# Four dense blocks in plain float32, merged complex products and moved reloads in a gated mix of an S4 convolution and a dense layer

## The chip, the core and the metric

The kernel runs on one core of a Trainium2 chip. Its engines are TensorE (PE), VectorE (DVE), ScalarE (ACT), GpSimd (POOL) and SyncE (SP); each runs its own instructions in order, and they wait for each other by semaphores. SP, ACT and POOL also issue transfers, which 16 DMA engines carry out. The metric is the device time of one execution in microseconds (us), the median of several.

## The reference

Two branches work on inputs of 2048 rows by 512 channels and are mixed by a gate for each row. Branch a is an S4 convolution: per channel a kernel K of 2048 taps is made from 128 complex modes and convolved with the input. Branch b is a dense layer of 512 to 1792 to 512 with a tanh gelu.

```python
dt = jnp.exp(log_dt)[:, None]
P = jnp.exp((dt * (A_re + 1j * A_im))[:, :, None] * l)       # 512 x 128 x 2048
K = jnp.einsum("dn,dnl,dn->dl", Cc, P, dt * Bc).real
a = causal_convolution(K, u) + u * Dskip                     # by rfft/irfft of length 4096
h = gelu(x @ w1 + b1)                                        # 2048 x 1792
b = h @ w2 + b2
g = sigmoid((u * gate_w).sum(-1, keepdims=True))
return g * a + (1 - g) * b
```

All is float32.

## The kernel before

The program has two parts. **The front** holds three streams. *Dense* (`hidden`, `output`): the 2048 rows are 8 tiles of 256 rows (`SB`), the 1792 hidden columns are 14 blocks of 128 in two halves of 7, and each tile is passed twice, once for each half; 64 steps in all. A matmul operand in float32 is split into a high half in float32r (`xh`, `wh`, `hh`: a cast by ACT or DVE) and a low half (`xlo`, `wl`, `hl`: a subtraction by DVE), and three products stand for one: high by high, low by high, high by low. The first weights wait in `sk` and `y`, buffers which the taps need later. `wh0`/`wl0` number k are the halves of the first layer's block k, `wh1`/`wl1` those of the second layer's. *Taps* (`prepare`, `coefficients`, `powers`, `magnitudes`, `rotate`, `contract`): powers of the modes are built by doubling in groups of 32 channels, 4 units of 4 groups, mostly on DVE, and contracted on PE; a first stage of the transform follows and the results go to DRAM (`tk_d`). *Signal*: the same first stage for the input, in 8 steps, to `tu_d`.

The order of the front is made by a small planner: each stream adds tasks with an engine, a length and what they read and write; a due number for each task decides which of the ready ones an engine takes next. The table `DUE` holds these numbers, the constants ahead of it shape the due times of the streams, and the planner's result is the order in which each engine's instructions stand in the program. `late` collects output products that are left for the second part.

**The convolution** (`conv`) comes after the front, in code order: 16 steps of `taps`, `signal`, `product`, `inverse`, `turn`. ACT copies the result of a step to `sa`, SP stores it to DRAM (`t4_d`), and after each 8 of the 32 slabs (a group) they are read back transposed into `den` and `t3`. Some of these reloads are held back in the list `held` and issued in a later step. `dense(k, queue)` reads a pair of tiles of the dense result back from DRAM, at the steps in `TIMES`, and `gated` multiplies it by its gate. At the end `rest` makes the leftover output products, and for each of eight tile pairs in `ORDER` the last matmuls (`pb`) are made from `den` or `t3`, added to the dense result and stored. PE reads tile pairs 0 and 1 from `den`, the others from `t3`; pairs 6 and 7 need the columns 16 to 24 of `t3`, pairs 4 and 5 the columns 8 to 16.

```python
if h == 24 and g < 2:
    held.append((t3[g:P:4, 16:24], rows[:, 24:32]))
    continue
if h > 8 and g == 2:
    held.append((t3[g:P:4, h - 8 : h], rows[:, h : h + 8]))
```

Of the kernel before, what the change touches and what calls it, by code (L numbers as in the profile page):

```python
# [33 lines left out]
T_0 = 30.908  # L34
T_MLP = 394.521
K_0 = 37.384
T_KG = 348.964
U_0 = 18.366
U_GAP = 16.805
LAG = 11.668  # L40
TABLE = 22.276
D_KA = -39.446
D_KP = 49.119
D_S1 = -141.104
D_EV = -12.266
D_H = -43.84
D_LO = -40.918
# [9 lines left out]
T_EARLY, T_LOFT, T_DEN = 111.918, -38.088, 66.187
Y_K, Y_U = 38.596, 37.383
W_MLP = (-0.038, -0.0445, 0.0156)
W_KG = (-0.0539, -0.0324, -0.0092)  # L60
W_U = (-0.0055, -0.1406, -0.0062)
D_MAG = -1.67
D_ROT = 0.254
D_CON = -215.721
D_PHA = 0.435
D_PRE = 0.748
D_XL = -38.576
D_COE = -209.658
D_OUT = -128.426
D_DTB = -9888.799  # L70
D_D0A = -91.29
D_LAST = -87.539
# [1 line left out]
D_KA0 = 171.664
D_DT = 8.244
D_PRM = -152.302
D_D0 = 46.196
D_WAVE0 = -326.561
D_COE0 = -59.569
D_SP1 = -888.307  # L80
D_G0 = 111.914
D_GW = 1362.531
D_XS0 = 96.565
T_PRE = 284.272
W_CAST = (0, 0, 0, 1, 1, 0, 1, 0, 0, 1, 0, 1, 0, 0)
# [1447 lines left out]
```

## Time and profile before

| | before |
|---|---|
| median of 3 runs | 504.18 us (502.92 to 505.89) |
| profiled execution, its own time | 504.54 us |
| its span | 502.8 us |
| busy: PE, DVE, ACT, POOL | 485.5, 426.9, 356.5, 71.4 us |
| DMA | 116.58 MB, mean 232 GB/s |
| granted TensorE clock, mean | 0.984 |

The span runs from the first instruction to the last; the profiled execution took 1.7 us more than it. A row of a timeline is start, length, engine, line of the program, operation, output and inputs, and in brackets the idle time before it and what ended that. SPq, ACTq are the sequencers of these engines, which issue transfers. A matmul's length is longer than the distance to the next one's start, since matmuls are pipelined. A plain float32 matmul shows as two rows. A row of a group has the number of instructions, the time they cover and the mean of one in ns.

### The profile page before, as it was taken

The numbers are of one execution on the slowest core, as the hardware profiler recorded it, in microseconds if no ns is written. First come the engines' busy times: TensorE is split into PE (matmuls) and PEld (weight loads), VectorE is DVE, ScalarE is ACT, GpSimd is POOL, SyncE is SP. The second block draws the span as 40 slices with busy tenths as digits, with TensorE's granted clock in tenths as the row PEclk, the third lists the DMA queues.
The fourth block names the chain that finished last, engine by engine and source line by source line (L and its number), as shares of the span: only waits on it lengthen the run. The fifth ranks groups of instructions, "written<-read, shape, count | busy, mean of one in ns | idle before, by whom it ended". The sixth has DMA issues, their size and how long they took to land.

```text
span 502.8 us, 12225 instructions
## 1 busy us (share of the span) xinstructions
PE 485.5 (97%) x4798; PEld 377.9 (75%) x4798; DVE 426.9 (85%) x793; ACT 356.5 (71%) x647; POOL 71.4 (14%) x115
## 2 busy tenths in 40 slices
PE   6999999999999999999999999999999989999976
PEld 5998898898898888989879888988988822223622
DVE  6999999999999999998999999999820269999234
ACT  4999768799884969977587996576533657889113
POOL 1012022101020101201221110011020040121003
PEclk8899999999999999999999999999999999999978
DMA  8977999955789625988973558795557999999867
GB/s 288 389 196 184 300 251 245 304 156 147 162 260 225 170 85 109 273 214 207 261 188 44 189 87 190 181 312 158 181 186 169 258 346 393 354 412 367 332 236 265
DMA packets 85001, 116.58 MB, mean 232 GB/s; under 512 B 39900, under 2 KB 41456, under 8 KB 84400
## 3 DMA queue, kind: packets, MB, share of 16 engines
q1 hardware_dynamic: 74880, 86.54, 53.5%
q0 software_dynamic: 9680, 27.04, 24.3%
q10 hardware_dynamic: 384, 2.23, 1.3%
q8 instruction: 37, 0.61, 0.5%
q14 instruction: 20, 0.16, 0.1%
HBM read 65.97 MB, written 49.81 MB: 230 GB/s over the span
## 4 chain that ended last, share of the span: by engine, by line
PE 60%; DVE 15%; DMA 9%; ACT 8%; issue 4%; SPq 3%; POOL 1%; DVEq 0%; ACTq 0%
PE pk L831 7%; PE ph L1023 7%; PE ph L1025 7%; PE ph L1024 6%; PE acc L1068 6%; PE p2k L1268 6%; PE acc L1069 5%; PE acc L1070 5%; PE pb L1426 3%; PE pa L1307 3%; DVE y L794 3%; DVE y L806 2%; PE p2u L1268 2%; DMA t_d<-sa 2%; PE ph L537 2%
## 5 line engine op out<-in xcount | busy, mean ns | idle before, releaser
L1023 PE MATMUL ph<-xh,wh 128*128 128x256 f32 x448 | 129.0, 288 | 3.1 <-ACT wh L932 3.0
L1025 PE MATMUL ph<-xh,wl 128*128 128x256 f32 x448 | 127.9, 286 | 0.9 <-DVE wl L934 0.9
L1024 PE MATMUL ph<-xlo,wh 128*128 128x256 f32 x448 | 127.7, 285 | 0.0
L1023 PEld LDWEIGHTS ph<-xh,wh 128*128 128x128 f32 x448 | 86.2, 192 | 9.5 <-issue 3.8
L1024 PEld LDWEIGHTS ph<-xlo,wh 128*128 128x128 f32 x448 | 86.3, 193 | 2.0
L1025 PEld LDWEIGHTS ph<-xh,wl 128*128 128x128 f32 x448 | 86.2, 192 | 1.4 <-DVE wl L934 1.4
L1068 PE MATMUL acc<-wh,hh 128*128 128x512 f32 x206 | 83.0, 403 | 0.0
L1069 PE MATMUL acc<-wl,hh 128*128 128x512 f32 x206 | 81.0, 393 | 0.0
L1070 PE MATMUL acc<-wh,hl 128*128 128x512 f32 x206 | 80.5, 391 | 0.0
L1040 ACT ACTIVATE ph<-ph,b1t 128x256 f32<-128x256 f32 x112 | 50.6, 452 | 32.4 <-PE ph L1025 30.5
L831 PE MATMUL pk<-y,den 128*32 128x64 f32 x2048 | 61.6, 290 | 0.1
L831 PEld LDWEIGHTS pk<-y,den 128*32 128x32 f32 x2048 | 57.2, 136 | 3.8 <-issue 2.1
L1053 DVE TENSOR_TENSOR hl<-ph,hh 128x512 fp32r<-128x512 f32 (+1 forms) x62 | 38.5, 622 | 24.3 <-ACT hh L1043 21.4
L1068 PEld LDWEIGHTS acc<-wh,hh 128*128 128x128 f32 x206 | 38.7, 188 | 18.6 <-issue 8.8
L794 DVE TENSOR_TENSOR y<-y,ea 128x64 f32<-128x64 f32 (+4 forms) x80 | 45.6, 570 | 1.4 <-ACT y L784 1.0
L1070 PEld LDWEIGHTS acc<-wh,hl 128*128 128x128 f32 x206 | 38.7, 188 | 8.7
L1069 PEld LDWEIGHTS acc<-wl,hh 128*128 128x128 f32 x206 | 38.7, 188 | 6.0
L1043 ACT CAST hh<-ph 128x512 fp32r<-128x512 f32 (+1 forms) x62 | 33.1, 533 | 13.7 <-PE acc L1069 11.9
L637 DVE TENSOR_TENSOR loft<-den,zz 128x256 f32<-128x256 f32 (+2 forms) x48 | 37.5, 780 | 0.2
L638 DVE TENSOR_TENSOR loft<-den,zz 128x256 f32<-128x256 f32 (+2 forms) x48 | 37.4, 779 | 0.1
L806 DVE TENSOR_TENSOR y<-y,loft 128x2048 f32<-128x2048 f32 x16 | 36.7, 2292 | 0.6 <-ACT loft L755 0.5
L1098 POOL DMA_DIRECT2D out_dram<-b2b x16 | 14.3, 913 | 100.8 <-DMA out_dram<-io 99.3
(188 smaller groups left out, 889.9 us busy)
## 6 DMA issues: line engine op xcount, KB each, us to landing
tu_d<-attic SPq DMA_DIRECT2D x64, 128.0 KB, 4.8
tk_d<-sk SPq DMA_DIRECT2D x32, 256.0 KB, 5.2
t_d<-sa SPq DMA_DIRECT2D x32, 256.0 KB, 5.7
tk<-tk_d SPq DMA_DIRECT2D x24, 256.0 KB, 5.0
t<-t_d POOLq DMA_DIRECT2D x9, 512.0 KB, 7.5
attic<-in_xt_dram SPq DMA_DIRECT2D x16, 256.0 KB, 5.2
xh_d<-xh SPq DMA_DIRECT2D x8, 512.0 KB, 5.9
xl_d<-xlo SPq DMA_DIRECT2D x8, 512.0 KB, 7.1
```

The lines of the kernel that those rows point to most:

```text
L794: nc.vector.tensor_mul(both(n, 64 - 3 * n, n), both(0, 64 - n, n), an)
L806: v.tensor_mul(y[:, 0].rearrange("p (a b) c -> p a b c", a=2), e.rearrange("p (a b) c -> p a b c", a=2), cc,)
L831: nc.tensor.matmul(pks[q][32 * j : 32 * j + 32, :, gg], x[:, r, :, ch], y[:, r, :, ch], start=(r == 0), stop=(r == 1), skip_group_check=True,)
L1023: nc.tensor.matmul(p, h, xh[xk][:, d], start=(d == 0), stop=False)
L1024: nc.tensor.matmul(p, h, xlo[xk][:, d], start=False, stop=False)
L1025: nc.tensor.matmul(p, lo, xh[xk][:, d], start=False, stop=(d == 3))
L1040: nc.scalar.activation(phs[q][:, n], phs[q][:, n], AF.Gelu_apprx_tanh, bias=b1t[:, f : f + 1])
L1053: nc.vector.tensor_sub(lo, phs[q][:, 0:nf], hi.bitcast(F32))
L1068: nc.tensor.matmul(a, h, wh[1][w], start=start, stop=False)
L1069: nc.tensor.matmul(a, h, wl[1][w], start=False, stop=False)
L1070: nc.tensor.matmul(a, l, wh[1][w], start=False, stop=(j == 3))
L1268: nc.tensor.matmul(out[64 * i : 64 * i + 64], w, x, start=True, stop=True)
```

## The change

1. *Plain float32.* For the first tile and the first four hidden blocks (`N_RAW = 4`), PE multiplies the loaded x and w1 as they are: 16 matmuls of 256 columns in float32 in place of 48 in float32r. The splits of these weights stay, since later tiles need them. The first weights of blocks 0 and 1 are loaded on ACT's queue.
2. *Merged products.* A complex product was four DVE operations (two products, a difference, a sum). `turned` makes it two, a product of twice the size and a sum of twice the size; for that `zz` is kept in four versions, two of which ACT copies (once as it is, once negated). `zz` moves to `shed`.
3. *Magnitudes from four powers.* ACT makes ten powers in `ea` where there were six, and copies seven columns to `y` where it was one; two of five doublings on DVE go.
4. *New front order.* New constants and a new `DUE`, now a plain sequence of ranks.
5. *Two reload pairs behind the loop.* The two held reloads of group 2, which POOL issued in steps 13 and 14, and the dense reads of the last two pairs (`THERE`), which SP issued in steps 13 and 14, go behind the loop, one pair on SP and one on ACT; the other dense reads come one or two steps earlier.

```diff
-TIMES = (5, 6, 7, 8, 10, 12, 13, 14)
+TIMES = (4, 5, 6, 7, 8, 10)
...
-    -100494, -3354, -2435, -1656, -1201, -1858, 2786, 719, 214, 1100, 242, -2033, -2824, 689, -3674, -3295, -2780,
+    1, 14, 16, 18, 20, 22, 24, 26, 30, 33, 41, 44, 47, 43, 79, 81, 93, 94, 99, 110, 119, 124, 128, 131, 136, 133, 4,
...
+        def turned(due, dst, a, b, n, t, ka, kd, kt):
+
+            w = a.shape[-1]
+            m = n * w
+            z = bass.AP(a.tensor, a.offset, [a.ap[0], [0, 2], *a.ap[1:]])
+            b = b.rearrange("p (b c) w -> p b c w", b=2).unsqueeze(3).to_broadcast([P, 2, 2, n, w])
+            t = t[:, : 4 * m].rearrange("p (b c n w) -> p b c n w", b=2, c=2, w=w)
+            v = t[:, 1, 1].copy()
+            v = bass.AP(v.tensor, v.offset, [v.ap[0], [-m, 2], *v.ap[1:]])
+            vec(4 * m, lambda: nc.vector.tensor_mul(t, z, b), due, [ka, "zz"], kt)
+            vec(2 * m, lambda: nc.vector.tensor_add(dst, t[:, 0], v), due, kt, [kd])
...
-                for k in range(11):
-                    e = ea[u % 2][:, k] if k < 6 else eb[:, k - 6]
-                    nc.scalar.activation(e, sc[:, 0], AF.Exp, scale=float(2**k))
+                for k, m in enumerate((32, 33, 34, 35, 3, 2, 1, 4, 8, 16, 64, 128, 256, 512, 1024)):
+                    e = ea[u % 2][:, k] if k < 10 else eb[:, k - 10]
+                    nc.scalar.activation(e, sc[:, 0], AF.Exp, scale=float(m))
...
+            def again():
+                nc.scalar.copy(zz[:, 1], zz[:, 0])
+                nc.scalar.mul(zz[:, 3], zz[:, 2], -1.0)
...
-                cmul(
-                    t, x[:, :, n : 2 * n], x[:, :, 0:n], zz[:, 0, i, cs], zz[:, 1, i, cs], n,
-                    xt_[:, :, 0:n], xv_[:, :, 0:n], ("xc", k), ["zz"], ("xc", k), "xt", "xv",
+                turned(
+                    t, x[:, :, n : 2 * n], x[:, :, 0:n], zz[:, :, i, cs], n,
+                    loft, ("xc", k), ("xc", k), ["xt", "xv"],
                 )
...
+            def copies():
+                nc.scalar.copy(e[:, 0:4], ea[u % 2][:, 0:4, cs])
+                nc.scalar.copy(e[:, 60:63], ea[u % 2][:, 4:7, cs])
...
-            for k in range(5):
+            for k in range(2, 5):
                 vec(2 * CW << k, lambda k=k: double(k), t, [("ea", u % 2)], ["y1"])
...
+            def plain(n, f):
+                for d in range(4):
+                    x, w = plainx[d // 2][0], rooms0[f][:, 0, d * P : (d + 1) * P]
+                    x = x[:, d % 2 * SB : d % 2 * SB + SB]
+                    nc.tensor.matmul(phs[q][:, n], w, x, start=(d == 0), stop=(d == 3))
...
+                if b == 0 and f < N_RAW:
+                    t_ = mm(
+                        1.74, lambda n=n, f=f: plain(n, f), t,
...
+            for f in range(2):
+                pl.add(
+                    "ACT", 0.4, lambda f=f: nc.scalar.dma_start(room[f][:, 0], w_rows(f, 0)), -3000 + f,
+                    [], [("room", f, 0)], lat=0.0, wire=(256 / 360.0, IN),
+                )
...
-            if s in (9, 10, 13, 14):
+            if s in (9, 10):
                 to, rows = held.pop(0)
                 nc.gpsimd.dma_start(to, rows)
...
             if s in TIMES:
-                dense((*HERE, *THERE)[TIMES.index(s)], nc.sync)
+                dense(HERE[TIMES.index(s)], nc.sync)
             if s > 9:
                 gated(HERE[s - 10])
+        for (to, rows), on, k in zip(held[::-1], (nc.sync, nc.scalar), THERE):
+            on.dma_start(to, rows)
+            dense(k, on)
```

How the instructions move is seen best in three places. Numbers behind a name are its buffer; `ph` holds hidden blocks before the gelu, `acc` output products, `attic` the loaded x, `sk` and `y` the loaded weights.

First, PE's row at its start, before: a warm-up, then the first hidden block in three products.

```order
L1526 UNCONDITIONAL_BRANCH
L1147 MATMUL pk0_91<-dm_147 128x128 x13
L1023 MATMUL ph0_88<-xh00_106,wh00_110 128x256
L1024 MATMUL ph0_88<-xlo00_108,wh00_110 128x256
L1025 MATMUL ph0_88<-xh00_106,wl00_124 128x256
```

The same place after:

```order
L1157 MATMUL pk0_91<-dm_146 128x128 x13
L1020 MATMUL ph0_88<-attic_76,sk_94 128x256 x8
L1020 MATMUL ph1_89<-attic_76,sk_94 128x256 x8
L1071 MATMUL acc1_87<-wh10_116,hh0_137 128x512
L1072 MATMUL acc1_87<-wl10_130,hh0_137 128x512
L1073 MATMUL acc1_87<-wh10_116,hl0_140 128x512
```

The four plain blocks stand first, and output products come directly behind them; before, five hidden blocks in three products stood ahead of the first output product.

Second, DVE's row at its start, before, behind the split of x:

```order
L934 TENSOR_TENSOR wl10_131<-sk_94,wh10_117 128x512
L612 TENSOR_TENSOR pr_101<-loft_77 128x128
L668 TENSOR_TENSOR pr_101<-pr_101 128x512
L934 TENSOR_TENSOR wl00_124<-sk_94,wh00_110 128x512
L673 TENSOR_SCALAR pr_101<-pr_101 128x128
L934 TENSOR_TENSOR wl01_125<-sk_94,wh01_111 128x512
L930 CAST wh11_118<-sk_94 128x512
L934 TENSOR_TENSOR wl11_132<-sk_94,wh11_118 128x512
```

After, from the end of the split of x on:

```order
L923 TENSOR_TENSOR xlo00_107<-attic_76,xh00_105 128x512
L923 TENSOR_TENSOR wl13_133<-sk_94,wh13_119 128x512
L586 CAST loft_77<-loft_77 128x128
L923 TENSOR_TENSOR wl11_131<-sk_94,wh11_117 128x512
L587 TENSOR_TENSOR pr_100<-loft_77 128x128
L919 CAST wh02_111<-sk_94 128x512
L655 TENSOR_TENSOR pr_100<-pr_100 128x512
L923 TENSOR_TENSOR wl02_125<-sk_94,wh02_111 128x512
L660 TENSOR_SCALAR pr_100<-pr_100 128x128
L1056 TENSOR_TENSOR hl0_140<-ph0_88,hh0_137 128x512
L919 CAST wh03_112<-sk_94 128x512
L923 TENSOR_TENSOR wl10_130<-sk_94,wh10_116 128x512
```

The splits of the first-layer weights 0 and 1 (wl00, wl01) now stand ahead of that of x, and wl10, which the second output product reads, is the last of these rows.

Third, SP's row at the end of the convolution, before:

```order
L1343 DMA loft_77<-out_0_dram 128x2x512
L1315 DMA t4_d_61<-sa4_4827 64x2x512
L1315 DMA t4_d_61<-sa5_4828 64x2x512
L1343 DMA loft_77<-out_0_dram 128x2x512
L1315 DMA t4_d_61<-sa0_4823 64x2x512
L1315 DMA t4_d_61<-sa1_4824 64x2x512
L1446 DMA out_0_dram<-attic_76 128x2x512 x3
```

After:

```order
L1325 DMA t4_d_61<-sa4_4690 64x2x512
L1325 DMA t4_d_61<-sa5_4691 64x2x512
L1325 DMA t4_d_61<-sa0_4686 64x2x512
L1325 DMA t4_d_61<-sa1_4687 64x2x512
L1419 DMA t3_4662<-t4_d_61 32x4096
L1353 DMA loft_77<-out_0_dram 128x2x512
L1459 DMA out_0_dram<-attic_76 128x2x512 x3
```

The last four stores have no dense read between them any more; a reload of group 2 and a dense read follow them.

ACT's row at the same place, before, with the reloads of the last group:

```order
L1313 COPY sa0_4823<-pa150_5416 128x512
L1313 COPY sa1_4824<-pa151_5419 128x512
L1330 DMA den_78<-t4_d_61 32x2048 x2
L1330 DMA t3_4799<-t4_d_61 32x4096 x3
L1349 ACTIVATE loft_77<-loft_77,gate_69 128x512 x2
```

After:

```order
L1323 COPY sa0_4686<-pa150_5275 128x512
L1323 COPY sa1_4687<-pa151_5278 128x512
L1340 DMA den_78<-t4_d_61 32x2048 x2
L1340 DMA t3_4662<-t4_d_61 32x4096 x3
L1359 ACTIVATE loft_77<-loft_77,gate_69 128x512 x2
L1419 DMA t3_4662<-t4_d_61 32x4096
L1353 DMA loft_77<-out_0_dram 128x2x512
```

The other held reload and the last dense read stand behind the five reloads of the last group.

More of the change, by code (lines that the diff above doesn't have):

```diff
@@ L33 @@
 NB = 2 * NSB
[L34 to L47, printed above, removed]
+T_0 = 33.369
+T_MLP = 397.0
+K_0 = 47.904
+T_KG = 342.331
+U_0 = 5.566
+U_GAP = 16.682
+LAG = 13.265
+TABLE = 0.0
+D_KA = -86.428
+D_KP = 95.084
+D_S1 = 29.729
+D_EV = -42.828
+D_H = -112.395
+D_LO = -48.166
 PS = (2, 3, 1, 2)
 N_ACC, N_H, N_PK, N_PU = PS
-D_SP = 5.602
-D_UL, D_UN, D_UA = -95.479, -24.453, -6.871
+D_SP = 21.319
+D_UL, D_UN, D_UA = -61.72, -46.925, -171.918
 MEM = (6, 2, 3)
 N_LD, N_HL, N_ST = MEM
-D_XS = 12.979
+D_XS = 21.116
 D_G = 2.936
 N_WARM = 13
[L57 to L72, printed above, removed]
-N_REST = 3
[L74 to L85, printed above, removed]
+T_EARLY, T_LOFT, T_DEN = 178.612, -1083.199, 54.393
+Y_K, Y_U = 27.579, 43.389
+W_MLP = (-0.0414, -0.046, 0.0184)
+W_KG = (-0.0406, -0.0643, 0.0065)
+W_U = (0.026, -0.1004, 0.0029)
+D_MAG = -21.881
+D_ROT = -73.254
+D_CON = -826.122
+D_PHA = -0.328
+D_PRE = 56.826
+D_XL = -13.443
+D_COE = -18.746
+D_OUT = -86.704
+D_DTB = -3780.088
+D_D0A = 19.191
+D_LAST = -7.801
+N_REST = 3
+D_KA0 = 22.676
+D_DT = 17.298
+D_PRM = -1055.059
+D_D0 = -39.205
+D_WAVE0 = -217.107
+D_COE0 = -75.159
+D_SP1 = -335.755
+D_G0 = 63.045
+D_GW = 739.44
+D_XS0 = 137.591
+T_PRE = 38.862
+W_CAST = (1, 0, 0, 0, 1, 1, 1, 0, 1, 0, 0, 0, 1, 1)
 X_CAST = (1, 1, 1, 1)
-D_X0, D_B2, D_B2A, D_DM = -2266.733, -4.442, -32.871, 35.72
+D_X0, D_B2, D_B2A, D_DM = -122.333, -53.659, 114.804, 136.838
 N_G = 9
+N_RAW = 4
 N_ATTIC, N_LOFT, N_TK = 11, 8, 10
@@ L297 @@
 TURN_PE = 0.095
-SLOW = 1.18
+SLOW = 1.0
 class Clock:
@@ L390, in run @@
                 took, (before, behind) = t.wire
-                wire = max(wire, at + before) + took * (SLOW if at > 22.0 else 1.6 if 3.2 < at < 4.2 else 1.15)
+                wire = max(wire, at + before) + took * (SLOW if at > 2.7 else 1.3)
                 end = wire + behind
@@ L457, in vec @@
         def vec(n, fn, due, reads=(), writes=(), fast=1):
-            return pl.add("DVE", 0.071 + n / 941.0 / fast, fn, due, reads, writes)
+            return pl.add("DVE", 0.064 + n / 952.0 / fast, fn, due, reads, writes)
         def act(n, fn, due, reads=(), writes=(), table=None, ops=1):
@@ L486, in front @@
         ph = pool.tile([P, 33, CW], I32, name="phase")
-        zz = pool.tile([P, 2, 5, UW], F32, name="zz")
+        zz = shed.rearrange("p k d -> p (k d)").rearrange("p (q k w) -> p q k w", q=4, w=UW)
         x4 = pool.tile([P, 2, 4, UW], F32, name="x4")
-        ea = tiles(2, [P, 6, UW], "ea")
+        ea = tiles(2, [P, 10, UW], "ea")
         pr = pool.tile([P, 7, UW], F32, name="pr")
@@ L583, in early @@
                 else:
-                    due, key = T_LOFT + m, ["xt", "xv"] if m < N_ATTIC + 4 else ["tt"] if m < N_ROOM else []
+                    due, key = T_LOFT + m, ["xt", "xv"] if m < N_ATTIC + 4 else ["tt"] if m < N_ROOM else ["zz"]
                 move(
@@ L712, in coefficients @@
             vec(5 * UW, lambda: v.tensor_mul(zz[:, 0], rr[:, 2:7], eb[:, 0:5]), t, ["xv", kx], ["zz"])
-            vec(5 * UW, lambda: v.tensor_mul(zz[:, 1], fr[:, 2:7], eb[:, 0:5]), t, ["xt", kx], ["zz"])
+            vec(5 * UW, lambda: v.tensor_mul(zz[:, 2], fr[:, 2:7], eb[:, 0:5]), t, ["xt", kx], ["zz"])
+            def again():
+                nc.scalar.copy(zz[:, 1], zz[:, 0])
+                nc.scalar.mul(zz[:, 3], zz[:, 2], -1.0)
+            act(10 * UW, again, t + D_KA, [], ["zz"], ops=2)
             t1, v1, wc = (eb[:, 2 * i : 2 * i + 2].unsqueeze(2) for i in range(3))
@@ L716, in coefficients @@
             cmul(t, x4[:, :, 0:1], wc, rr[:, 1], fr[:, 1], 1, t1, v1, kx, ["xt", "xv"], "x4", kx, kx)
-            cmul(
-                t, x4[:, :, 1:2], x4[:, :, 0:1], zz[:, 0, 0], zz[:, 1, 0], 1, t1, v1,
-                "x4", ["zz"], "x4", kx, kx,
-            )
-            t2, v2 = (
-                z.rearrange("p a b c -> p (a b c)")[:, : 4 * UW].rearrange(
-                    "p (a b c) -> p a b c", a=2, b=2
-                )
-                for z in (xt_, xv_)
-            )
-            cmul(
-                t, x4[:, :, 2:4], x4[:, :, 0:2], zz[:, 0, 1], zz[:, 1, 1], 2, t2, v2,
-                "x4", ["zz"], "x4", "xt", "xv",
-            )
+            turned(
+                t, x4[:, :, 1:2], x4[:, :, 0:1], zz[:, :, 0], 1,
+                eb.rearrange("p a w -> p (a w)"), "x4", "x4", [kx],
+            )
+            turned(t, x4[:, :, 2:4], x4[:, :, 0:2], zz[:, :, 1], 2, loft, "x4", "x4", ["xt", "xv"])
         def phases(c, t):
@@ L771, in powers @@
                 n = 1 << i
-                cmul(
-                    t, x[:, :, n : 2 * n], x[:, :, 0:n], zz[:, 0, i, cs], zz[:, 1, i, cs], n,
-                    xt_[:, :, 0:n], xv_[:, :, 0:n], ("xc", k), ["zz"], ("xc", k), "xt", "xv",
+                turned(
+                    t, x[:, :, n : 2 * n], x[:, :, 0:n], zz[:, :, i, cs], n,
+                    loft, ("xc", k), ("xc", k), ["xt", "xv"],
                 )
@@ L783, in magnitudes @@
             pl.add("GP", 0.13, lambda: nc.gpsimd.memset(e[:, 63], 1.0), t + D_KA, [], ["y1"])
-            act(CW, lambda: nc.scalar.copy(e[:, 0], ea[u % 2][:, 5, cs]), t + D_KA, [("ea", u % 2)], ["y1"])
+            def copies():
+                nc.scalar.copy(e[:, 0:4], ea[u % 2][:, 0:4, cs])
+                nc.scalar.copy(e[:, 60:63], ea[u % 2][:, 4:7, cs])
+            act(7 * CW, copies, t + D_KA, [("ea", u % 2)], ["y1"], ops=2)
             def both(lo, step, n):
@@ L1025, in products @@
                     nc.tensor.matmul(p, lo, xh[xk][:, d], start=False, stop=(d == 3))
+            def plain(n, f):
[3 more added lines that the diff above has]
+                    nc.tensor.matmul(phs[q][:, n], w, x, start=(d == 0), stop=(d == 3))
             for n, f in enumerate(fs):
                 w = f % FH
+                if b == 0 and f < N_RAW:
+                    t_ = mm(
+                        1.74, lambda n=n, f=f: plain(n, f), t,
+                        [("room", f, 0), *(key for _, key in plainx)], [("h", q)], turn="f32",
+                    )
+                    for k in [("sk", c, j) for c in range(2) for j in range(4)] if f < 4 else ("y0", "y1"):
+                        pl.readers[k].append(t_)
+                    continue
                 mm(
@@ L1105, in output @@
                         add(n, r, t)
-        kept = []
+        kept, plainx, rooms0 = [], [], []
         def add(n, r, t):
@@ L1132, in dense @@
             room = [sks[:, f] if f < 4 else ys[:, f - 4] for f in range(FH)]
+            plainx.extend(x)
+            rooms0.extend(room)
+            for f in range(2):
+                pl.add(
+                    "ACT", 0.4, lambda f=f: nc.scalar.dma_start(room[f][:, 0], w_rows(f, 0)), -3000 + f,
+                    [], [("room", f, 0)], lat=0.0, wire=(256 / 360.0, IN),
+                )
             for f in range(FH):
-                for r in range(2):
+                for r in range(f < 2, 2):
                     move(
@@ L1211, in front @@
         for t, due in zip(pl.tasks, DUE, strict=True):
-            t.due = due / 10
+            t.due = due
         for t in pl.run():
```

4 lines of the change are left out of this document (2 added, 2 removed), and 154 rows, old and new, of the table DUE.

## The prediction

> **What bounds the kernel now.** I read the page's busy times first, then the busy time by stretch, then who waited for whom, and then the timeline of the stretches where TensorE is not full.
>
> ```profile
> span 502.8 us, 12225 instructions
> PE 485.5 (97%) x4798; PEld 377.9 (75%) x4798; DVE 426.9 (85%) x793; ACT 356.5 (71%) x647; POOL 71.4 (14%) x115
> PEclk8899999999999999999999999999999999999978
> ...
> 6.00:9.20 3.20, 0.25 (x3) 0.06 (x1) 3.05 (x10) 1.24 (x2) 0.70 (x2) 0.91 1.04 383
> 9.20:15.60 6.40, 5.67 (x25) 5.37 (x26) 6.33 (x13) 5.37 (x22) 0.00 (x0) 0.51 1.05 383
> 15.60:40.00 24.40, 24.40 (x171) 22.39 (x177) 23.86 (x58) 23.87 (x35) 1.83 (x2) 1.00 0.77 253
> 40.00:100.00 60.00, 60.00 (x650) 51.06 (x638) 59.46 (x118) 45.56 (x80) 11.86 (x16) 1.00 0.97 268
> 100.00:200.00 100.00, 99.59 (x1161) 87.04 (x1154) 96.44 (x177) 82.77 (x154) 10.97 (x18) 1.00 0.65 165
> 200.00:300.00 100.00, 99.57 (x1185) 85.36 (x1184) 95.43 (x190) 81.81 (x147) 16.56 (x26) 1.00 0.74 185
> 300.00:400.00 100.00, 100.00 (x1092) 88.94 (x1091) 69.14 (x112) 56.10 (x99) 9.81 (x16) 1.00 0.75 199
> ...
> PE pb L1426 <- DMA den<-t_d: 4.3, 1, 4.3
> ...
> PE p2k L1268 <- POOL f L1251: 1.6, 1, 1.6
> ```
>
> In a stretch's row the columns are its length, the busy time of PE, weight loads, VectorE, ScalarE and GpSimd, then granted clock, DMA share and GB/s. From 15.6 to 400 us PE lacks 0.84 us in all, at full clock: there TensorE is the bound, and a shorter VectorE instruction buys nothing. What can be won lies in three places: the first 15.6 us (PE late, then at half clock), the start of the convolution at 400 us (1.6 us), and the end (4.3 us of waiting, with a half clock behind it).
>
> **The start: four blocks in plain float32.**
>
> ```profile
> GB/s 0 0 0 83 97 197 296 242 300 398 351 262 358 361 367 410 410 397 402 401 398 393 356 348 356 401 397 393 390 366 370 385 393 401 442 406 389 377 352 258
> ...
> 1.19 5.06 PE L1147 MATMUL pk<-dm 128*128 128x128 f32 x26 [1.19 <-POOL dm L1142]
> 7.80 2.02 ACT L932 CAST wh<-sk 128x512 fp32r<-128x512 f32 x3 [3.67 <-DMA sk<-in_w_dram]
> 9.21 0.58 PE L1023 MATMUL ph<-xh,wh 128*128 128x256 f32 x1 [2.97 <-ACT wh L932]
> 10.73 0.58 PE L1025 MATMUL ph<-xh,wl 128*128 128x256 f32 x1 [0.72 <-DVE wl L934]
> 15.47 0.42 DVE L930 CAST wh<-sk 128x512 fp32r<-128x512 f32 x1
> 15.64 0.28 PE L1024 MATMUL ph<-xlo,wh 128*128 128x256 f32 x1
> 15.76 0.28 PE L1025 MATMUL ph<-xh,wl 128*128 128x256 f32 x1
> 15.81 0.69 DVE L934 TENSOR_TENSOR wl<-y,wh 128x512 fp32r<-128x512 f32 x1
> 16.41 0.69 DVE L934 TENSOR_TENSOR wl<-sk,wh 128x512 fp32r<-128x512 f32 x1
> ...
> 487.29 10.49 PE L1426 MATMUL pb<-t,g1t 128*64 128x512 f32 x52
> ```
>
> *Price on PE.* A float32r matmul of 256 columns starts every 0.12 us (15.64, 15.76), so the 48 removed ones are 5.8 us. Plain float32: the last row covers six tile pairs of the end, 12 times 512 columns by a pair of 64-wide halves that run together, 0.87 us each; 256 columns of a full-width weight are then 0.44, sixteen of them 7.0 us. The change costs PE 1.2 us here.
>
> *When it can begin.* The first row is GB/s in half microseconds; summed, 1.34 MB has moved by 6.6 us. That is the step constants, x, the parameters, c1 and the first weight of before, which ScalarE could use at 7.80: landing costs 1.2 us more. After, the two first weights go out on ScalarE's queue and x on SyncE's; both x halves and both weights are done at about 1.21 MB, 6.3 us, so usable at 7.5, against 9.21 and 10.73 for the first products of before. PE would end the four blocks at 14.5.
>
> *What then holds it.* The output products that follow need the split of the second weights. On VectorE the order now has, from the first split (possible once the first weight has landed, about 5.7, and ScalarE has cast it, 6.3) to the low half wl10 that the second output matmul reads: ten 512-wide operations of 0.60 us (15.81 to 16.41), five casts of 0.34 (15.47 to 15.81), nine 128-wide ones that I put at 0.25, an estimate: 9.9 us, and 0.3 for a weight not yet there: 16.5. PE idles 1.8 us. By the same count it waits 0.9 us for wl06 and 1.2 us for wl05. So the seven hidden blocks and 24 output matmuls of the first tile (24 at 0.23, 36 at 0.12) end at 14.5 + 1.8 + 5.5 + 4.3 + 2.1 = 28.2 us. Before, 25 matmuls (3.0 us of full-clock work) were done at 15.6, and the other 12.6 us of the same work ran unbroken: 28.0. The start is worth 0: the earlier PE runs into VectorE, which splits the same weights and has two casts more. Bounds: 4.4 us gained if VectorE kept up (all waits gone); lost 1.2 us if the half clock comes back: the warm-up ends at 6.25, and in before the gap from there to 9.21 brought 0.51 from 9.2 on. Of that gap 1.25 us would be left. As long a half clock as before's (9.2 to 15.6) would end the four blocks 3.2 us later, at 17.7, 1.2 us behind wl10. I take 0, since more than half of the gap is gone.
>
> The Trainium skill (TensorE: Matmul & The Clock Gate, Part 1: The HAM clock gate) says that the gate falls to half after an idle window of about 3.4 us, and that the window is free-running. A gap of 2.96 us was enough here, so the trace is the stricter of the two; by the rule full clock stays and the sum is the same 0, with a half clock it would be the 1.2 us more.
>
> **Merged products, four powers.**
>
> ```profile
> L637 DVE TENSOR_TENSOR loft<-den,zz 128x1024 f32<-128x1024 f32 x16 | 19.6, 1225 | 0.2
> ...
> L637 DVE TENSOR_TENSOR loft<-den,zz 128x512 f32<-128x512 f32 x16 | 11.1, 692 | 0.1
> ```
>
> Doubling 512 elements adds 533 ns, so 159 ns of an operation are fixed. Each of the 56 products goes from four operations to two with the same elements: 112 x 0.159 = 18 us at most; counted by starts (0.60 for 0.69) 7 us. Two doublings fewer in 16 magnitudes save 32 short ones, 5 to 8 us. ScalarE gets 16 exponentials, 8 long copies and 16 more copies, some 12 us, at 71% busy. All of it is off PE's path (the rows above): 0, with 1.5 us either way for the new order. The switches between the two matmul kinds are 32 in both orders.
>
> **Start of the convolution.**
>
> ```profile
> 400.84 0.18 POOL L1120 COPY look<-xh 128x1 f32<-128x1 f32 x1 [23.78 <-ACT xh L1043]
> 401.15 1.72 POOL L1112 DMA_DIRECT2D out_dram<-io  x2
> 403.01 0.88 POOL L1250 TENSOR_SCALAR f<-cc 32x256 f32<-32x256 f32 x1
> 405.77 1.08 PE L1268 MATMUL p2k<-tk,f 128*64 128x512 f32 x4 [1.63 <-POOL f L1251]
> ```
>
> PE waits for matrices that GpSimd makes after two accumulating stores, which wait for a cast. In the new order one more pair of output products stands behind that cast, so it is done some 1.4 us sooner relative to PE's last hidden block, but the stores then wait for two copies behind it: GpSimd gains 0.5 us. I take 0.5; bounds 0 and 1.6.
>
> **The end.**
>
> ```profile
> 462.81 1.05 POOL L1399 DMA_DIRECT2D t<-t_d  x2
> 467.22 1.17 SPq L1315 DMA_DIRECT2D t_d<-sa  x2
> 476.60 0.39 PE L1362 MATMUL acc<-wh,hl 128*128 128x512 f32 x1
> 478.13 1.15 ACTq L1330 DMA_DIRECT2D den<-t_d  x2
> 481.25 6.22 PE L1426 MATMUL pb<-den,g1t 128*64 128x512 f32 x16 [4.26 <-DMA den<-t_d]
> ...
> 445.00:450.00 5.00, 5.00 (x40) 1.17 (x31) 5.00 (x9) 3.53 (x8) 2.62 (x5) 1.00 1.10 422
> 465.00:470.00 5.00, 5.00 (x25) 3.31 (x24) 0.86 (x2) 1.43 (x3) 0.00 (x0) 1.00 1.02 378
> 470.00:475.00 5.00, 5.00 (x23) 4.13 (x22) 0.99 (x2) 0.00 (x0) 0.00 (x0) 1.00 0.95 362
> 481.00:485.00 4.00, 3.75 (x10) 1.38 (x12) 0.78 (x2) 1.33 (x2) 0.00 (x0) 0.50 1.00 348
> ...
> t_d<-sa SPq DMA_DIRECT2D x32, 256.0 KB, 5.7
> ```
>
> The last stores are issued at 467.2, and the reload that needs them can go only at 478.13: 11 us, against a median of 5.7, because the DMA engines are full (share about 1). The change takes two reloads (2 x 0.52 MB) and two loads of the dense result (the same) out from ahead of them: 2.1 MB at 370 GB/s (mean of 378 and 362) is 5.7 us. The stores land at 472.4, or 473.5 by the median; I take 473. The first slab came 3.1 us after its issue (478.13 to 481.25): 476.1, before PE ends its leftover products (476.99, less 0.5). So the wait of 4.26 us goes, and with it the half clock (0.50): two tile pairs took 6.04 us (481.25 to 487.29) where the next six took 1.75 each, 2.5 us more. PE: 476.5 + 8 x 1.75 = 490.5, and as before 5.0 us to the end (497.78 to 502.8): 495.5. Late next is the DMA: from 472.4 on it must move 4.2 MB of reads and 4.2 MB of results, 8.4 MB at 370, 22.7 us, to 495.1, and about 1 us to close: 496.1, which I take. ScalarE's fifth and later reloads wait for landings on shared semaphores, which at these rates are there.
>
> The Trainium skill (DMA: Bandwidth & Descriptors, Specifications) gives about 358 GB/s as HBM's limit for a core. By it the end would be at 496.9 and the time 0.8 us more; the trace shows 422 for 5 us, so the measurement decides.
>
> **Sum.** Span 502.8 - 6.7 = 496.1; the profiled execution took 504.54, so 497.8 against itself. It lies 0.36 above the median of the runs: 497.5. About 0.5% (2.5 us) is what a measurement of this kernel can tell from no change.
>
> **Rivals.**
> 1. *The start opens.* VectorE's early operations overlap with transfers that come sooner on two queues, and PE never waits: 4.4 us more, 493.1. For it: VectorE idles until the first weight is cast, so each microsecond of landing passes straight on. Against: 9.9 us of operations in a row. 0.15.
> 2. *The new front order makes PE wait* 2 to 4 us between 28 and 400 us: VectorE was 95 to 100% busy up to 300 us, and the first signal stage stands some 20 us earlier in PE's row (matmuls of 35 us ahead of it, by the prices above, against 55), so its chain of loads, negation and accumulating transfers must be through sooner. 500.5. Against: VectorE has at least 12 us less to do. 0.17.
> 3. *The stores land no sooner* (the change doesn't do what it says): share was about 1 since 400 us, and other traffic fills the room. Then 8.4 MB start at 478.1, at 348 GB/s 24.1 us, and 1 us: 503.3, time 505.0 - 0.4 = 504.6. Against: 2.1 MB do leave. 0.12.
> 4. *Slower.* The second half of the slabs lands late: writes and reads share the engines, and ScalarE's queue holds its fifth reload until SyncE's moved one has landed. PE stands after four tile pairs (483.5); if for 6 us, the gate halves the clock for the other four, 4 x 1.27: 501.6 + 5.0, time 508. It decides from a wait of 4.7 us on. For it: 348 GB/s at share 1.00. 0.06.
>
> **How the numbers follow.** The forecast (495.5 to 499.5) has 0.50. Faster by over 0.5% (under 501.7): it, rival 1 and most of rival 2: 0.80; the same: rest of 2, and 3: 0.13; slower: 4 and a little of 3: 0.07. The range 493.5 to 502.0 leaves out rivals 3 and 4 and the far edge of 1, 0.2.
>
> **What would show it.** Right: the first plain block at 7 to 8 us; PE waiting for VectorE's wl at about 14.5; 400 us reached within 1.5 us of before; the reload issued within 6 us of the last store; no wait above 1 us at the first pb, clock 1.00 to the end. Wrong: PE waits of microseconds in the middle; the reload at 10 us again; gaps between the fourth and fifth tile pair.

## The result, and the profile after

The changed kernel takes 500.14 us (median of 14 runs, 496.3 to 502.6) where the kernel before took 505.79 us beside it (502.9 to 510.9): ratio 0.9887, 95% interval 0.9866 to 0.9908, or 5.7 us less (4.7 to 6.8). The forecast was 497.5, a gain of 6.7 from 504.18, in a range of 493.5 to 502.0. The sum came out near, in part by luck: three of its terms did not, and they erred to opposite sides. The profiled execution of the changed kernel took 501.5 us.

Three lines of its page: the span, the busy times and the granted clock in 40 slices. The dents at both ends of the clock's row are gone.

```profile
span 499.7 us, 12099 instructions
PE 482.9 (97%) x4782; PEld 375.2 (75%) x4782; DVE 415.2 (83%) x651; ACT 366.9 (73%) x685; POOL 70.9 (14%) x113
PEclk9999999999999999999999999999999999999999
```

Busy time by stretch, columns as before (length, PE, weight loads, VectorE, ScalarE, GpSimd, clock, DMA share, GB/s):

```profile
6.00:9.20 3.20, 3.20 (x21) 2.97 (x20) 3.20 (x11) 1.93 (x4) 0.77 (x1) 1.00 1.05 378
9.20:15.60 6.40, 6.40 (x31) 5.57 (x30) 6.40 (x16) 5.53 (x15) 0.00 (x0) 1.00 1.06 387
15.60:40.00 24.40, 23.84 (x165) 20.31 (x164) 24.27 (x57) 24.06 (x48) 2.64 (x4) 1.00 0.95 294
40.00:100.00 60.00, 58.77 (x694) 50.04 (x696) 57.52 (x85) 47.60 (x81) 10.27 (x15) 1.00 0.83 229
100.00:200.00 100.00, 100.00 (x1103) 87.16 (x1094) 94.90 (x142) 86.90 (x173) 11.98 (x20) 1.00 0.71 184
200.00:300.00 100.00, 96.97 (x1094) 82.89 (x1097) 86.65 (x138) 79.93 (x150) 15.63 (x24) 1.00 0.75 182
300.00:400.00 100.00, 100.00 (x1172) 88.86 (x1161) 69.10 (x87) 59.91 (x107) 10.90 (x18) 1.00 0.73 188
...
480.00:485.00 5.00, 5.00 (x26) 2.00 (x24) 3.66 (x5) 0.85 (x2) 0.70 (x1) 1.00 1.02 338
```

From 6 to 15.6 us PE is full at full clock, where before it was idle and then at half. But from 15.6 to 400 us it now lacks 4.8 us (0.56, 1.23 and 3.03), where 0.84 were missing before. Who PE waits for says where (in total, times, longest):

```profile
PE pk L820 <- DVE y L806: 2.4, 1, 2.4
...
PE p2k L1278 <- POOL f L1261: 1.2, 1, 1.2
PE ph L1012 <- issue: 1.2, 1, 1.2
PE ph L1012 <- DVE hl L1056: 0.8, 2, 0.6
PE pa L1317 <- ACT sa L1323: 0.7, 1, 0.7
PE ph L1014 <- DVE wl L923: 0.4, 2, 0.2
...
PE pb L1439 <- DMA den<-t_d: 0.2, 1, 0.2
```

The wait at the end is down from 4.3 to 0.2 us; the largest is new, 2.4 us for the taps. The timeline of the two ends (start, length; several answers, in order of time):

```profile
2.27 5.11 PE L1157 MATMUL pk<-dm 128*128 128x128 f32 x26 [2.27 <-POOL phase L877]
...
4.00 0.62 ACT L921 CAST wh<-sk 128x512 fp32r<-128x512 f32 x1 [1.05 <-DMA sk<-in_w_dram]
4.65 0.69 DVE L923 TENSOR_TENSOR wl<-sk,wh 128x512 fp32r<-128x512 f32 x1 [0.40 <-ACT wh L921]
...
7.21 7.07 PE L1020 MATMUL ph<-attic,sk 128*128 128x256 f32 x32
13.94 0.58 PE L1071 MATMUL acc<-wh,hh 128*128 128x512 f32 x1
14.35 0.39 PE L1072 MATMUL acc<-wl,hh 128*128 128x512 f32 x1
...
465.55 5.84 SPq L1325 DMA_DIRECT2D t_d<-sa  x4
475.70 1.15 ACTq L1340 DMA_DIRECT2D den<-t_d  x2
478.86 3.65 PE L1439 MATMUL pb<-den,g1t 128*64 128x512 f32 x16 [0.19 <-DMA den<-t_d]
482.32 10.50 PE L1439 MATMUL pb<-t,g1t 128*64 128x512 f32 x52
```

The warm-up ends at 7.38 us (2.27 and 5.11). The four plain blocks run from 7.21 to 13.94 us, and the output products follow almost at once. At the end the first two tile pairs take 3.46 us (478.86 to 482.32) in place of 6.04.

### The profile page after: what moved, and what is told of

Read it like the earlier page. It is cut to its first block, busy times and chain, and to the rows that moved or that the text cites. A ratio compares the mean times of both kernels' runs of the same rounds, so it can differ in the third digit from the quotient of the medians.

```text
span 499.7 us, 12099 instructions
## 1 busy us (share of the span) xinstructions
PE 482.9 (97%) x4782; PEld 375.2 (75%) x4782; DVE 415.2 (83%) x651; ACT 366.9 (73%) x685; POOL 70.9 (14%) x113
## 4 chain that ended last, share of the span: by engine, by line
PE 77%; DVE 9%; DMA 7%; ACT 3%; issue 2%; POOL 1%; POOLq 0%; SPq 0%; DVEq 0%; ACTq 0%
PE pk L820 12%; PE ph L1012 9%; PE ph L1014 8%; PE ph L1013 8%; PE acc L1071 8%; PE acc L1072 8%; PE acc L1073 8%; PE p2k L1278 5%; DMA attic<-in_xs_dram 3%; PE pa L1317 3%; PE pb L1439 3%; PE ph L512 3%; PE p2u L1278 2%; DVE wl L923 2%; DMA t_d<-sa 1%
## 5 line engine op out<-in xcount | busy, mean ns | idle before, releaser
L1012 PE MATMUL ph<-xh,wh 128*128 128x256 f32 x432 | 123.3, 285 | 2.0 <-issue 1.2
L1014 PE MATMUL ph<-xh,wl 128*128 128x256 f32 x432 | 122.3, 283 | 0.4 <-DVE wl L923 0.4
L1013 PE MATMUL ph<-xlo,wh 128*128 128x256 f32 x432 | 122.2, 283 | 0.0
L1012 PEld LDWEIGHTS ph<-xh,wh 128*128 128x128 f32 x432 | 82.0, 190 | 7.1 <-issue 3.5
L1013 PEld LDWEIGHTS ph<-xlo,wh 128*128 128x128 f32 x432 | 82.1, 190 | 2.1 <-DVE xlo L923 0.2
L1014 PEld LDWEIGHTS ph<-xh,wl 128*128 128x128 f32 x432 | 82.1, 190 | 0.8 <-DVE wl L923 0.8
L626 DVE TENSOR_TENSOR loft<-den,shed 128x512 f32<-128x512 f32 (+2 forms) x48 | 67.1, 1399 | 0.2
L1056 DVE TENSOR_TENSOR hl<-ph,hh 128x512 fp32r<-128x512 f32 (+1 forms) x62 | 38.4, 619 | 29.1 <-ACT hh L1046 28.9
L1071 PEld LDWEIGHTS acc<-wh,hh 128*128 128x128 f32 x206 | 38.7, 188 | 20.2 <-issue 10.3
L783 DVE TENSOR_TENSOR y<-y,ea 128x256 f32<-128x256 f32 (+2 forms) x48 | 37.3, 777 | 2.7 <-ACT y L771 2.4
L627 DVE TENSOR_TENSOR den<-loft 128x256 f32<-128x256 f32 (+2 forms) x48 | 37.3, 777 | 0.2
L720 DVE CUSTOM_DVE_ANT_0 phase<-phase 128x128 uint16<-128x128 uint16 (+1 forms) x64 | 25.9, 405 | 0.5
```

Of the source, the lines that this page charges most:

```text
L626: vec(4 * m, lambda: nc.vector.tensor_mul(t, z, b), due, [ka, "zz"], kt)
L627: vec(2 * m, lambda: nc.vector.tensor_add(dst, t[:, 0], v), due, kt, [kd])
L783: nc.vector.tensor_mul(both(n, 64 - 3 * n, n), both(0, 64 - n, n), an)
L1012: nc.tensor.matmul(p, h, xh[xk][:, d], start=(d == 0), stop=False)
L1013: nc.tensor.matmul(p, h, xlo[xk][:, d], start=False, stop=False)
L1014: nc.tensor.matmul(p, lo, xh[xk][:, d], start=False, stop=(d == 3))
```

## The experiments

All times, each against the kernel before on the same chip (its median was 505.5 to 507.2 us). `after_again`, `gate_again` and `gate_no_tail` ran on one chip, `tail_undone`, `tail_only`, `no_plain` and `gate_moved` on a second, the other four on a third; between chips, compare the ratios:

| kernel | median us | ratio to before (95%) |
|---|---|---|
| changed, again (`after_again`) | 500.03 | 0.9884 (0.9845 to 0.9923) |
| changed, end of before (`tail_undone`) | 504.33 | 0.9954 (0.9932 to 0.9977) |
| before, new end (`tail_only`) | 501.85 | 0.9916 (0.9883 to 0.9948) |
| changed, no plain blocks (`no_plain`) | 503.79 | 0.9949 (0.9926 to 0.9973) |
| changed, row sum moved (`gate_moved`) | 497.42 | 0.9823 (0.9789 to 0.9858) |
| the same again (`gate_again`) | 498.29 | 0.9844 (0.9801 to 0.9886) |
| row sum moved, end of before (`gate_no_tail`) | 502.76 | 0.9931 (0.9903 to 0.9958) |
| row sum moved, warm-up sooner (`both`) | 497.95 | 0.9816 (0.9761 to 0.9870) |
| changed, products unmerged (`unmerged`) | 502.24 | 0.9927 (0.9890 to 0.9963) |
| changed, only held reloads moved (`held_only`) | 501.55 | 0.9884 (0.9821 to 0.9947) |
| changed, two dense reads left out (`no_reread`) | 498.63 | 0.9831 (0.9752 to 0.9911) |

From the traces: first product of the convolution (the end of the front), issue of the loop's last store, ScalarE's first reload, first `pb`, end of PE, span.

| trace | front ends | last store | reload | first pb | PE ends | span |
|---|---|---|---|---|---|---|
| before | 400.56 | 467.84 | 478.13 | 481.25 | 497.78 | 502.8 |
| `before_again` | 405.08 | 472.36 | 483.86 | 487.02 | 503.53 | 508.5 |
| `tail_undone` | 400.54 | 467.63 | 478.46 | 481.56 | 497.46 | 502.4 |
| `gate_no_tail` | 399.27 | 466.15 | 476.84 | 479.99 | 496.04 | 501.0 |
| after | 401.63 | 469.56 | 475.70 | 478.86 | 492.82 | 499.7 |
| `after_again` | 400.77 | 468.15 | 473.46 | 477.19 | 491.15 | 497.2 |
| `tail_only` | 404.82 | 473.63 | 479.65 | 482.76 | 496.72 | 503.8 |
| `gate_moved` | 398.48 | 465.36 | 470.79 | 474.42 | 488.59 | 494.7 |
| `gate_again` | 398.32 | 467.87 | 473.66 | 476.91 | 491.24 | 497.7 |
| `both` | 399.15 | 466.02 | 471.94 | 475.32 | 489.52 | 496.3 |
| `unmerged` | 403.37 | 470.24 | 476.20 | 479.31 | 493.73 | 500.1 |
| `no_plain` | 404.53 | 472.12 | 477.56 | 481.65 | 495.61 | 501.3 |
| `held_only` | 399.96 | 468.80 | 476.67 | 479.75 | 493.95 | 498.8 |
| `no_reread` | 399.89 | 466.77 | 472.76 | 475.94 | 490.50 | 495.9 |

**What the end is worth, from both sides.** `tail_undone` is the changed kernel with:

```diff
-TIMES = (4, 5, 6, 7, 8, 10)
+TIMES = (5, 6, 7, 8, 10, 12, 13, 14)
-            if s in (9, 10):
+            if s in (9, 10, 13, 14):
-                dense(HERE[TIMES.index(s)], nc.sync)
+                dense((*HERE, *THERE)[TIMES.index(s)], nc.sync)
-        for (to, rows), on, k in zip(held[::-1], (nc.sync, nc.scalar), THERE):
-            on.dma_start(to, rows)
-            dense(k, on)
```

> The changed kernel with the end of before: the two held reloads and the two dense reads go back into steps 13 and 14. Theory (the whole gain is at the end): the stores land late again, PE waits 3 to 5 us at the first pb and two tile pairs run at half clock, so about 6 us are lost against the changed kernel: ratio to before 0.998 to 1.003, and the end of the front stays about 1 us later than before's 400.6. Rival (the end is bound by the bytes that the DMA engines must move, whatever their order, and the gain came from the start): at most 2 us are lost, ratio 0.989 to 0.993.

`tail_only` is the reverse of this diff on the kernel before.

> The kernel before with nothing but the two reload pairs behind the loop (and the six earlier dense reads). Theory: 5 to 6.5 us faster than before, ratio 0.987 to 0.990, as fast as the changed kernel or faster, since the front ends at 400.6 and not at 401.6; reload issued within 6.5 us of the last store, no wait above 0.5 us at the first pb, clock 1.00 to the end. Rival (new front and new end are both needed): 2 us faster, ratio 0.996.

Undoing the end loses 0.67% (3.4 us, by the two intervals some 1.6 either way) of the changed kernel's gain; the end alone wins 0.84% (4.3 us, interval 2.6 to 5.9). The waits and the timeline of `tail_undone` show before's end again, the reload 10.8 us after the last store and half a clock behind the wait (two tile pairs in 5.42 us):

```profile
PE pb L1436 <- DMA den<-t_d: 5.0, 1, 5.0
```

```profile
478.46 1.15 ACTq L1340 DMA_DIRECT2D den<-t_d  x2
...
481.56 5.59 PE L1436 MATMUL pb<-den,g1t 128*64 128x512 f32 x16 [5.00 <-DMA den<-t_d]
486.98 5.33 PE L1436 MATMUL pb<-t,g1t 128*64 128x512 f32 x24
```

In `tail_only` the reload goes 6.0 us after the last store and the first `pb` waits 0.03 us. So the mechanism works on either front, but for less than predicted, and neither theory's number was met for `tail_undone`: it stays 2.3 us (1.2 to 3.4) faster than before, although its front ends at 400.54, where the first trace of before has 400.56. The trace of `tail_only`, with before's front, ends it at 404.82. Its waits show why:

```profile
PE pu L537 <- ACT attic L561: 1.2, 1, 1.2
PE acc L1068 <- ACT hh L1043: 1.1, 1, 1.1
```

These two, at 57.9 and 60.1 us, are in no row of before's first trace, and 3.4 us of half clock follow them. That led to the next run, before once more:

> A second trace of the kernel before. Theory (the first trace was one of its good executions; another profile with the same front had PE waiting 1.2 and 1.1 us at 58 and 60 us with 3.4 us of half clock behind): the front ends 1 to 4 us later than 400.6. Rival (the first trace was typical): within 0.5 us of it.

```profile
PE pb L1426 <- DMA den<-t_d: 5.5, 1, 5.5
PE ph L1023 <- ACT wh L932: 4.2, 1, 4.2
...
PE ph L537 <- DVE hl L1053: 1.1, 1, 1.1
```

Its front ends at 405.08, and this execution took 510.5 us. The long wait at the start is not why: the half clock behind it is shorter (3.4 us instead of 6.8), and the first tile's seven hidden blocks and 24 output products are done at 28.5 us, against 28.3 in the first trace. The rest builds up between 150 and 350 us, in several steps of about 1 us and less. The prediction was read from the best of three executions of before's front: 400.56, 404.82, 405.08. The two late ones are not typical either: 510.5 us is longer than all 17 other executions of before beside it (503.5 to 509.2), and the profiled one of `tail_only` (505.6) is the longest of its 11. The changed front ends between 399.89 and 401.63 in five traces (mean 400.56).

The end again, on a quieter front (row sum moved, below):

> The moved row sum together with the end of before. Its distance to the kernel with the moved row sum alone is what the end is worth on a front without the wait of 2.4 us. Theory (the end is worth what the traces show from the first product of the convolution on, 102 us against 97.3): 4.7 us between the two, this one at 0.991 to 0.993. Rival (it is worth the 6.2 us that were predicted): 0.994 to 0.996. Rival (3.4 us, the distance of the two medians so far): 0.989.

502.76 against 498.29 (the same chip) and 497.42: 4.5 to 5.3 us. From the end of the front to the end of the span, the four traces with the old end take 102.3 us on average (101.7 to 103.4), eight with the new one 97.5 (96.2 to 99.4): 4.8 us. With like fronts it is 4.6 on the new one (two traces against seven) and 3.8 on before's (two against one). The theory held, though the interval of its ratio reaches into the rival of 6.2 us.

**The wait of 2.4 us in the middle.** SyncE's, VectorE's and PE's side of it in the changed kernel, by the timeline:

```profile
228.97 4.11 SPq L914 DMA_DIRECT2D attic<-in_xs_dram  x1
...
229.53 1.22 DVE L802 SCALAR_TENSOR_TENSOR y<-y,loft 128x1024 f32<-128x1024 f32 x1
234.61 0.69 DVE L967 SCALAR_TENSOR_TENSOR attic<-attic 128x512 f32<-128x512 f32 x1 [3.86 <-DMA attic<-in_xs_dram]
...
235.22 1.22 DVE L806 TENSOR_TENSOR y<-y,loft 128x1024 f32<-128x1024 f32 x1
...
236.59 0.67 PE L820 MATMUL pk<-y,den 128*32 128x64 f32 x16 [2.43 <-DVE y L806]
```

L967 is a row sum for the gate, which is applied only in the convolution, 200 us later. Its x, on SyncE's queue among stores, lands at 234.6, and L806, the last operation before the taps' product, stands behind it: VectorE idles 3.86 us and PE 2.43. `gate_moved` exchanges the two on VectorE and moves nothing else:

```diff
-        for t in pl.run():
+        order = pl.run()
+        k = [n for n, t in enumerate(order) if t in sums][13]
+        n = next(n for n in range(k, len(order)) if order[n] in turns)
+        order.insert(n, order.pop(k))
+        for t in order:
             t.fn()
```

(`sums` holds the row sums, `turns` the L806 of each group.)

> The changed kernel with one VectorE operation moved: the row sum of the gate that waits for its x (3.86 us at 234.6) goes behind the last operation of the taps' group (L806), on which PE waited 2.43 us at 236.6. Theory: that wait of PE falls under 0.3 us and 2.3 us are gained, 0.984. Rival 1 (VectorE only comes late later): PE waits as long a few us on, 0.988 to 0.989. Rival 2 (the lead is given back in the convolution, which the transfers bound): the front ends 2.3 us sooner, the span does not.

```profile
229.17 1.23 DVE L806 TENSOR_TENSOR y<-y,loft 128x1024 f32<-128x1024 f32 x1
232.63 0.69 DVE L967 SCALAR_TENSOR_TENSOR attic<-attic 128x512 f32<-128x512 f32 x1 [2.23 <-DMA attic<-in_xs_dram]
...
232.58 3.84 PE L820 MATMUL pk<-y,den 128*32 128x64 f32 x128
```

PE runs through; VectorE still waits 2.23 us for the load, and PE doesn't wait with it. The front ends at 398.5, 2 us sooner than the mean of the changed front, and the time falls to 497.42: this version beats both kernels.

> The kernel with the moved row sum once more, on the same chip as the changed kernel. Theory: 2.5 to 3.2 us faster than it (the wait of 2.4 us, and in some executions the half clock behind it), 0.981 to 0.984. Rival (the first distance came from the chip): within 1 us of it.

Beside `after_again` (below) it is 1.7 us faster, less than expected but beyond the rival's 1 us. The two intervals against before overlap (0.9801 to 0.9886 and 0.9845 to 0.9923), but four of its five times lie below all six of `after_again`.

> The changed kernel once more, for a second trace and for a comparison on the chip of the next two. Expected: 0.987 to 0.991; the front ends between 399.9 and 401.7, PE waits 2.3 to 2.7 us at 236, in some executions with 3.4 us of half clock behind it.

The second trace has the same wait, 2.45 us at 236, and no half clock behind it.

**The start.** `no_plain` sets `N_RAW = 0`. Besides the 48 products in place of the four plain blocks, the planner then moves some two dozen of PE's 2,300 rows; twelve of them, a fifth hidden block, go from 17 us to the start.

> The changed kernel with the first four hidden blocks in three float32r products again, all due numbers kept (the planner moves some rows of the first microseconds). Theory (plain blocks let PE begin before x is split): the first product can go at 9.2, when the second low half of x is done (9.15 in the trace), PE idles 1.8 us behind the warm-up; the four blocks end at 15.0 where plain ones ended at 13.9, +1 us at full clock, and +3 to 4 us where the gap brings the half clock of before: ratio 0.991 (full clock) or 0.996 (half). Rival, as predicted (VectorE bounds the first 16 us, the start is worth nothing): within 0.5 us of the changed kernel, 0.988 to 0.990.

Its timeline, its busy time by stretch and two of its waits:

```profile
7.15 0.38 PE L1012 MATMUL ph<-xh,wh 128*128 128x256 f32 x1 [0.16 <-DVE xh L919]
7.95 0.39 PE L1013 MATMUL ph<-xlo,wh 128*128 128x256 f32 x1 [0.42 <-DVE xlo L923]
```

```profile
9.20:15.60 6.40, 5.73 (x44) 5.32 (x44) 6.37 (x16) 3.85 (x10) 0.00 (x0) 1.00 1.06 388
15.60:40.00 24.40, 21.71 (x142) 17.74 (x140) 22.37 (x54) 23.95 (x48) 2.67 (x4) 1.00 0.84 278
```

```profile
PE ph L1012 <- ACT attic L536: 1.7, 1, 1.7
...
PE ph L1012 <- DVE hl L1056: 1.0, 1, 1.0
```

It loses 0.62% (3.1 us), more than the expected 1 us, and in another place. PE begins at 7.15 with what is split by then, not at 9.2, and the clock stays full: the half clock of before's start is gone without plain blocks too, since the warm-up now ends where the products begin. What is lost are 2.69 us between 15.6 and 40 us (0.56 in the changed kernel), 1.0 of it at 30.7 us, where PE has caught up with VectorE's split of a hidden block (hl), and 1.7 us at 40.9 for a copy by ScalarE. The first tile's seven hidden blocks and 24 output products are done at 26.6 us, against 24.8 in the changed kernel and 28.3 in before: half of what the start gained comes without plain blocks. How much of the loss is the moved rows is open.

`both` adds to `gate_moved` that dm, which the warm-up multiplies, is cleared first on GpSimd.

> The kernel with the moved row sum, and the clearing of dm moved to the head of GpSimd's order, so that the warm-up of PE starts at 1.2 us and not at 2.27 and ends at 6.3. Theory (the warm-up holds the first plain block): the block starts at 6.3 to 6.6 and 0.7 to 1.0 us are gained, 0.980 to 0.981. Rival (x and the weights land at 7): it starts where it did, 0.982 to 0.983; with a gap that brings the half clock back, 0.987.

```profile
6.50 7.07 PE L1020 MATMUL ph<-attic,sk 128*128 128x256 f32 x32
13.22 0.58 PE L1071 MATMUL acc<-wh,hh 128*128 128x512 f32 x1
14.18 0.50 PE L1072 MATMUL acc<-wl,hh 128*128 128x512 f32 x1 [0.38 <-DVE wl L923]
```

The plain blocks start at 6.50 as expected, and the 0.7 us are given back at the second output product, which waits for wl10: 14.18 in place of 14.35. The time is that of `gate_moved`. So VectorE does bound the start, but only from about 14 us on.

**Merged products.** `unmerged` gives each `turned` its four operations back, at the same places:

```diff
-            vec(4 * m, lambda: nc.vector.tensor_mul(t, z, b), due, [ka, "zz"], kt)
-            vec(2 * m, lambda: nc.vector.tensor_add(dst, t[:, 0], v), due, kt, [kd])
+            def four():
+                nc.vector.tensor_mul(t[:, 0], a, b[:, 0])
+                nc.vector.tensor_mul(t[:, 1], a, b[:, 1])
+
+            def two():
+                nc.vector.tensor_add(dst[:, 0], t[:, 0, 0], t[:, 1, 1])
+                nc.vector.tensor_add(dst[:, 1], t[:, 0, 1], t[:, 1, 0])
+
+            vec(4 * m, four, due, [ka, "zz"], kt)
+            vec(2 * m, two, due, kt, [kd])
```

> The changed kernel with each merged complex product of the powers made by four VectorE operations again (112 more, same elements, at the same places of the order; ScalarE still makes the two copies of zz). VectorE's busy time goes from 415 to some 425 to 433 us. Theory (the waits of PE in the front come from single late operations, not from VectorE's total): within 1.5 us of the changed kernel, 0.986 to 0.992. Rival (VectorE at 95 to 100% up to 300 us hands every microsecond on): 4 us slower or more, 0.996 and up.

VectorE's busy time goes from 415.2 to 422.3 us, so merging saves 7 us there, the prediction's count by starts and less than the 10 to 18 expected here. The ratio, 0.9927, is between the two theories and its interval overlaps the changed kernel's; the trace has one more wait (0.56 us at 161), a half clock of 3.4 us behind the wait at 238, which the traces of the changed kernel don't have, and a front that ends at 403.37. Whether merging is worth 0 or 2 us is not settled.

**Which bytes count at the end.** `held_only` leaves only the two held reloads behind the loop (`TIMES` gets 13 and 14 for the last two dense reads).

> The changed kernel with only the two held reloads behind the loop; the dense reads of the last two pairs are issued on SyncE's queue in steps 13 and 14 as before. Theory (every byte in front of the last stores counts the same, 1.05 of 2.1 MB are back): reload about 8 us after the last store, half of the end's gain lost, 0.991 to 0.993. Rival 1 (the reads stand in SyncE's own queue ahead of the stores and are what holds them): all lost, 0.995. Rival 2 (GpSimd's reloads were what held them): nothing lost, 0.988 to 0.990.

```profile
476.67 1.15 ACTq L1340 DMA_DIRECT2D den<-t_d  x2
...
479.75 3.65 PE L1438 MATMUL pb<-den,g1t 128*64 128x512 f32 x16 [1.84 <-DMA den<-t_d]
```

The reload comes 7.9 us after the last store (6.1 in the changed kernel, 10.8 in `tail_undone`), as the theory of equal bytes has it; the interval of the ratio is too wide to tell the three apart, and only just leaves out rival 1 (0.995).

`no_reread` passes `dense` a flag that leaves out the two reads behind the loop (1.05 MB), so two tile pairs miss their dense part.

> The changed kernel without the dense reads of the last two tile pairs (1.05 MB behind the loop; these two pairs of the output then have a wrong dense part). Theory (the last 25 us are bound by the bytes that the DMA engines move): the last transfer ends 2.6 to 2.8 us sooner relative to the last store of the loop, 0.983. Rival (PE's end and the landing of its last store bound it): PE's end and the span stay, 0.988 to 0.990.

From the loop's last store to the end of the span it takes 29.1 us against a mean of 29.7 in the eight traces with the new end (29.1 to 30.3), and from PE's end on 5.4 against 6.4 (5.7 to 7.1). `held_only`, which has no dense read behind the loop either, takes 4.8 from PE's end on. So the bytes do not cost 2.7 us. That they cost 0.6 to 1 us, with PE bounding most of the end and the transfers its last microsecond, is what these two traces suggest; one of the two figures lies within the spread of the others. The ratio's interval is too wide to add anything.

## Why the prediction was right and wrong

*The start (predicted 0, bounds 4.4 gained to 1.2 lost): wrong.* The seven hidden blocks and 24 output matmuls of the first tile, put at 28.2 us, are done at 24.8 (28.3 in before's first trace): 3.4 us gained. When the first plain block begins (7.5 predicted, 7.21), its price (0.44 a matmul, 0.42) and the end of the four (14.5, 13.94) were right. The step that failed is "possible once the first weight has landed, about 5.7, and ScalarE has cast it, 6.3": I had shared one stream's bytes over all transfers, but the weight goes out first on its own queue; ScalarE casts it at 4.00 and VectorE splits at 4.65. The 9.9 us of operations took 9.4, wl10 was there shortly after 14 and not at 16.5, and the waits of 1.8, 0.9 and 1.2 us became some 0.2 each. That is rival 1, with its own mechanism. But not all of the 3.4 us is the plain blocks': without them (`no_plain`) the same work is done at 26.6. The full clock came, but not for the reason given: the warm-up began at 2.27 us instead of 1.19, since GpSimd clears dm later, and so reached to the first block, where a gap of 1.25 us was expected. That was luck.

*Merged products and new order (predicted 0, 1.5 either way): wrong in size.* Rival 2 came true as well: PE waits 4.8 us in the front of the profiled execution, against 0.84. The place was not the first signal stage, as I had it, but a row sum in front of the taps' last operation; with it moved, the time fell by 1.7 us (same chip) to 3.2 (by the ratios to before). In this trace nothing was left of the start's 3.4 us at 400 us: 401.63 against 400.56.

*Start of the convolution (0.5): right.* GpSimd's matrices are waited for 1.25 us instead of 1.63.

*The end (6.2): right in mechanism, too large.* The reload goes 6.1 us after the last store (10.3 before; 5.3 to 6.1 in the eight traces), the first `pb` waits 0.2 us, the clock stays full, PE takes 14.0 us for the eight tile pairs: much as predicted. From the end of the front on, 6.7 us were predicted, with the 0.5 of the convolution's start, and 4.8 came by the traces; the medians give 3.4 to 5.3 for the end. Two sizes were off. After PE's end it takes 6.4 us on average and not 5.6; that the reads behind the loop push back the last results fits `no_reread` (5.4) and `held_only` (4.8), one trace each. And from the end of the front to the first `pb` it takes 76.9 us and not 75.9 (476.5 less 400.56): in five of these eight traces PE waits 0.5 to 1.6 us in all for ScalarE's copies to `sa`, whose buffers are freed by the stores, and in the three without that wait it takes 75.9 to 76.2. Rivals 3 and 4 did not come.

*The base.* The sum stood on one trace of before, whose front was 4 us better than in its other two; those two were among the slowest executions, and before's medians (505.5 to 507.2) lie 1 to 2.7 us above the execution that I read. By the medians the changed front is worth 2.3 us (1.2 to 3.4, `tail_undone`), though nothing against the trace that I read. So 500.14 is within the range, with a start that won more than foreseen, an order that lost that again, and an end that won less.
